# Local attention beside a state-space scan on one core: first tokens loaded in pairs, weight rows loaded twice, 64-row parts paired, one rotation more on VectorE, the last block in halves, and a new order

## The chip, the core and the metric

The kernel runs on one core of a Trainium2 chip. The core has TensorE (PE; its weight loads are listed apart as PEld), VectorE (DVE), ScalarE (ACT), GpSimd (POOL) and SyncE (SP), which here only issues DMAs. The metric is the device time of one execution in microseconds.

## The reference

Two independent parts take their own input of 2048 tokens by 448 features (bf16), and their results stand side by side in the output (2048 x 896).

```python
# A: dilated local attention, 16 heads of 28, window 8, dilation 2
qkv = x @ wqkv                                  # 448 x 1344
logits[s, w] = q[s] . k[s - 2 w] * 28 ** -0.5   # w = 0..7, masked where s - 2 w < 0
o[s] = sum_w softmax(logits[s])[w] * v[s - 2 w]
a = o @ wo
# B: a diagonal complex recurrence (S5)
Lam_bar = exp(dt * Lam);  Bu = x @ (((Lam_bar - 1) / Lam)[:, None] * Bmat).T
h[t] = Lam_bar * h[t - 1] + Bu[t]
b = 2 * real(h @ Cmat.T) + x * Dskip
out = concat(a, b)
```

## The kernel before

**The order.** Every piece of work is a small Python function ("step") with a name and arguments. The string `ORDER` lists all steps by hand, and the loop at the end of the kernel calls them one after the other. A step appends its instructions to the queues of the engines that it uses; within an engine instructions run in that order, and between engines semaphores hold a reader until its input is there and a writer until the old content has been read. `@` and digits give the banks of PSUM (eight, 0 to 7) that a step writes; `.` and `=` at the end say whether a copy out of PSUM (an eviction) runs on ScalarE or VectorE. So `qk010.` is the eviction of step `qk` for u=0, m=1, s=0 on ScalarE. DMAs stand in SP's queue in the same way, ScalarE's three small ones aside; SP stops at a DMA whose input is not ready.

**Part A.** x is brought to `xT` (features on partitions): tokens 0 to 1023 (u=0) by TensorE, `XI` for the first 512 and `XA`, `XH` for the next, with evictions `xi`, `xa`, `xh`; tokens 1024 to 2047 (u=1) by transposing DMAs. 448 features are three chunks of 128 and one of 64. The 64-row chunk of two 512-token halves s=0, 1 lies on partitions 0 to 63 and 64 to 127, so its weights are needed on both: the load brings them to partitions 0 to 63, and POOL copies them to the others and gathers the last heads' columns in `wq6` (lines 213 to 218). `QK(u, m, k)` projects to queries (even m) and keys (odd m) for both halves: k=0 the three full chunks, k=1 the two 64-row parts as a pair on the two halves of the array. `QS(m, s)` does all four chunks of one half, with one 64-row matmul by itself. `qk` and `qh` evict to `qf`, `kf`, `qh_t`, `kh`. `V_`/`v` do the same for the values. `P` forms products of queries and shifted keys on VectorE (24 of `pr<-qf,kf`, 4 of `pr<-qh_t,kh`); `E_` sums them over a head by a matmul with 32 columns of weights; `lt`, `TR`, `tr`, `sma`, `smb`, `smc` are scaling, transpose and softmax; `AL`, `al`, `ad`, `sp` spread the probabilities into a band `PT` through DRAM; `AV`, `av`, `W_`, `w`, `ow` are the weighted sum, the output projection and its store.

**Part B.** Tokens are grouped in fours (T = 4, j = 0..3), states in seven groups g of 64 (real and imaginary part on 128 partitions). `tf`, `ts`, `pa` to `pg`, `rb` compute tables and rotation matrices `R`. `BU` (input projection) and `BR` (adds the step before, rotated) fill PSUM; `z` evicts; `UP`, `sa`, `sb`, `sd`, `DN`, `dn` do the scan over groups of four tokens. Its carry then goes into the tokens j = 0..2 by one of two ways: `H_(j, g)` rotates it on TensorE and `h` adds it on VectorE (12 pairs of j, g), or `sw` copies it across partitions by DMA and `ha`, `hb` (or `ka`, `kb`, the same instructions) rotate and add it on VectorE (9 pairs). `C(j, ct)` multiplies 128 tokens by the output matrix (seven matmuls of 448 columns), `c` adds `x * Dskip`, `oc` stores. The order ends with C01, C02 and the store oc02.

Changes of the array: a weight of 128 rows by 128 columns, of 64 rows, or of 32 columns uses TensorE in different shapes, and the order decides how often the shape changes.

Of the kernel before, what the change touches and what calls it, by code (L numbers as in the profile page):

```python
# [9 lines left out]
BF16 = mybir.dt.bfloat16  # L10
# [5 lines left out]
HALO = 14  # L16
# [21 lines left out]
qh000. qh011. v000= qh101. QK110@70 P010 E_00@4 qh001. E_02 E_04 xt3 ts13 QK111 P031 QK121@31 qh100. QK141@65 qh111.
QK140 hc0 qk111. ts23 qk141. ts25 QK120 qk140. qk120. QK100@05 qk121. P050 qk110. V_410@63 hc1 qh110. QK101 P061 P011
qk100. qk101. V_411 E_01@1 tf2 ts02 P051 LC P030 E_03 tf6 E_05 QK130@72 P060 E_06 QK151@05 v411. v410. QK131 qk130.  # L40
P101 qk131. P111 lt00 P110 QK150 qk151. V_500@36 V_501 qk150. V_511@72 lt01 P131 v501. V_401@45 TR0@0 V_400 ts06 V_510
E_11@1 tr0. P100 v500. v401. v400. v511. v510. P130 E_13 E_10@6 sma0 smb0 P121 P141 BU401@03 OZ P150 BU201@54 BU301@27
# [20 lines left out]
def kernel(  # L63
# [68 lines left out]
    def qk_load(c, n):  # L132
        for a in range(2):
            SP.dma_start(qk_s[:, 0:3, a, c:c + n], qk_d[0:384, a, c:c + n].rearrange("(f p) n -> p f n", p=128))
        SP.dma_start(qk_s[0:64, 3, :, c:c + n], qk_d[384:448, :, c:c + n])
# [784 lines left out]
```

## Time and profile before

| | |
|---|---|
| three runs | 131.55 to 131.69 us, median 131.67 |
| the profiled execution | 131.66 us, of which the span of its instructions 129.9 us |
| busy in the span | PE 123.9 us, DVE 119.0, ACT 90.9, PEld 62.8, POOL 23.0 |
| DMA | 22.91 MB in 44838 packets, 31064 of them under 512 bytes |
| first matmul, end of the last one | 1.06 us, 126.5 us |

Rows of the timeline give start, length, engine, source line, operation, the tile written and read, the shape and the count; in brackets the idle time before and what ended it. Lengths of matmuls overlap, so the cost of one in a dense row is the distance from start to start. Groups give the busy time and the mean length of one in ns. The chain of waits is followed back from the last instruction. SPq is SP's queue with DMA issues.

### The profile page before, as it was taken

How to read it: one execution, taken by the hardware profiler on the slowest of the kernel's cores; microseconds unless marked ns; L12 is line 12 of the kernel's file. 1: busy time of each engine (PE TensorE's matmuls, PEld its weight loads, DVE VectorE, ACT ScalarE, POOL GpSimd, SP SyncE). 2: the span in 40 equal slices, each digit the busy share in tenths (PEclk: the TensorE clock that was granted, in tenths of full speed). 3: DMA queues.
4: the chain of work that ended last, by engine and by line, in shares of the span. 5: the costliest groups of instructions: out<-in, count | busy, mean ns of one | idle time of the engine just before them, and what ended most of it. 6: DMA issues, size and time to landing. Idle time of an engine off the chain costs nothing.

```text
span 129.9 us, 2872 instructions
## 1 busy us (share of the span) xinstructions
PE 123.9 (95%) x1071; PEld 62.8 (48%) x1071; DVE 119.0 (92%) x211; ACT 90.9 (70%) x185; POOL 23.0 (18%) x45
## 2 busy tenths in 40 slices
PE   6899999999989999999999999999999999999990
PEld 6843445343423434435446335945694554555540
DVE  5679999999999999999999999999999999999941
ACT  3459899999974999987999987999889651000000
POOL 6817300000000000003999900000000000000000
PEclk9999999999999999999999999999999999999999
DMA  3899998999999979973577699995512430124463
GB/s 99 196 315 270 308 214 166 229 221 237 167 204 213 226 192 343 240 136 71 203 186 138 273 259 239 209 153 91 184 29 89 110 129 6 34 71 139 144 208 110
DMA packets 44838, 22.91 MB, mean 176 GB/s; under 512 B 31064, under 2 KB 43800, under 8 KB 44824
## 3 DMA queue, kind: packets, MB, share of 16 engines
q1 hardware_dynamic: 44760, 22.72, 74.8%
q8 instruction: 8, 0.13, 0.4%
q14 instruction: 7, 0.05, 0.1%
q10 hardware_dynamic: 63, 0.01, 0.0%
HBM read 11.56 MB, written 6.29 MB: 137 GB/s over the span
## 4 chain that ended last, share of the span: by engine, by line
PE 57%; DVE 28%; ACT 9%; issue 3%; DVEq 0%
PE ps L238 21%; DVE pr L378 13%; PE ps L831 13%; PE ps L524 4%; PE ps L701 4%; PE ps L511 3%; DVE Ak L796 3%; PE ps L256 2%; PE ps L347 2%; DVE Z L800 2%; DVE Z L772 2%; ACT kh L114 2%; ACT qf L114 1%; DVE Cw L667 1%; ACT qh_t L114 1%
## 5 line engine op out<-in xcount | busy, mean ns | idle before, releaser
L378 DVE TENSOR_TENSOR pr<-qf,kf 128x2048 bf16<-128x2048 bf16 x24 | 28.4, 1231 | 0.0
L238 PE MATMUL ps<-xbuf,BT 128*128 128x512 bf16 (+1 forms) x112 | 24.0, 379 | 0.0
L831 PE MATMUL ps<-Cw,Z 128*128 128x448 bf16 x112 | 21.8, 352 | 0.1
L238 PE MATMUL ps<-xT,wq 128*128 128x512 bf16 (+1 forms) x96 | 19.7, 380 | 0.0
L114 ACT CAST Z<-ps 128x512 bf16<-128x512 f32 (+1 forms) x34 | 15.7, 503 | 0.9 <-PE ps L713 0.5
L831 PEld LDWEIGHTS <-Z 128*128 128x128 bf16 x112 | 11.0, 98 | 10.5 <-issue 0.3
L238 PEld LDWEIGHTS <-BT 128*128 128x128 bf16 (+1 forms) x112 | 9.1, 97 | 11.7 <-issue 2.4
L524 PE MATMUL ps<-wo,oT 128*128 128x448 bf16 x64 | 13.6, 353 | 0.0
L238 PEld LDWEIGHTS <-wq 128*128 128x128 bf16 (+1 forms) x96 | 7.5, 97 | 11.5 <-issue 4.0
L238 PE MATMUL ps<-wq,xT 128*128 128x448 bf16 (+1 forms) x64 | 12.0, 353 | 0.0
L877 POOL MEMSET PT<- 128x4320 f32 x3 | 11.0, 3699 | 0.0
L837 DVE TENSOR_TENSOR xbuf<-ps,xnB 128x448 bf16<-128x448 f32 x16 | 9.2, 619 | 2.0 <-PE ps L831 1.7
L114 ACT CAST oT<-ps 128x512 bf16<-128x512 f32 x17 | 9.5, 626 | 1.4 <-PE ps L511 1.4
L114 ACT CAST ya<-ps 128x448 bf16<-128x448 f32 (+1 forms) x17 | 8.4, 557 | 2.8 <-issue 1.6
L663 ACT ACTIVATE ctmp<-Cw,c2t 64x448 f32<-64x448 bf16 x14 | 9.3, 666 | 0.3
L114 ACT CAST kf<-ps 128x512 bf16<-128x512 f32 x12 | 6.8, 596 | 3.5 <-PE ps L238 2.5
L524 PEld LDWEIGHTS <-oT 128*128 128x128 bf16 x64 | 6.1, 98 | 5.7 <-ACT oT L114 0.6
L511 PE MATMUL ps<-PT,v_s 128*32 128x135 bf16 (+1 forms) x256 | 8.4, 299 | 0.0
L238 PEld LDWEIGHTS <-xT 128*128 128x128 bf16 (+1 forms) x64 | 5.3, 97 | 5.5 <-issue 1.1
L772 DVE TENSOR_TENSOR Z<-ps,Z 128x512 bf16<-128x512 f32 x12 | 7.9, 682 | 0.0
L114 ACT CAST v_s<-ps 128x448 bf16<-128x448 f32 x15 | 7.3, 541 | 0.5 <-PE ps L238 0.5
L511 PEld LDWEIGHTS <-v_s 128*32 128x32 bf16 x256 | 7.1, 112 | 0.2 <-issue 0.2
(159 smaller groups left out, 197.0 us busy)
## 6 DMA issues: line engine op xcount, KB each, us to landing
PT<-pd SPq DMA_DIRECT2D x16, 156.0 KB, 4.0
xnB<-in_B_x_dram SPq DMA_DIRECT2D x2, 896.0 KB
out_dram<-ya SPq DMA_DIRECT2D x16, 112.0 KB, 1.7
out_dram<-xbuf SPq DMA_DIRECT2D x16, 112.0 KB, 1.7
pd<-Ak SPq DMA_DIRECT2D x2, 640.0 KB, 3.2
xbuf<-in_A_x_dram SPq DMA_DIRECT2D x2, 448.0 KB
xnB<-in_B_x_dram SPq DMA_DIRECT2D x4, 224.0 KB, 6.0
xnB<-in_B_x_dram SPq DMA_DIRECT2D x4, 192.0 KB, 4.4
```

The lines of the kernel that those rows point to most:

```text
L114: (ACT.copy if e == "A" else V.tensor_copy)(o, i)
L238: PE.matmul(o, l, r, start=(first and i == 0), stop=(not first and i == len(pairs) - 1 and not more[s]))
L378: V.tensor_tensor(t[:], q.unsqueeze(1).to_broadcast((128, 4, 512)), k4, ALU.mult)
L511: PE.matmul(p[32 * hh:32 * hh + 32, 128 * bl:128 * bl + n], v_s[:, t, 4 * hg + hh, :], PT[:, t % NS, (4 * hg + hh) // HS, (4 * hg + hh) % ...
L524: PE.matmul(p[:, 0:D], late["oT"][:, b // 4, hg, par, 128 * (b % 4):128 * (b % 4) + 128], late["wo"][:, hg, :], start=(hg == 0), stop=(hg ...
L663: ACT.activation(t[a:a + 64, 0:D], Cw[b:b + 64, g, :], ACTF.Copy, scale=c2t[a:a + 64, g:g + 1])
L701: PE.matmul(pp["z", g, j][:], rot(g, 0), late["Z"][:, g, j - 1, :], start=False, stop=True)
L772: V.tensor_tensor(zz, pp.pop(("h", j, g))[:], zz, ALU.add)
L796: e.scalar_tensor_tensor(t.rearrange("p (a n) -> p a n", a=2), prev(g), co2[:, 0, j, g:g + 1], late["Z"][:, g, j, :].rearrange("p (a n) -> ...
L831: PE.matmul(p[:, 0:D], z, Cw[:, g, :], start=(g == 0), stop=(g == G - 1))
L837: V.tensor_tensor(yo, pp.pop(("c", j, ct))[:, 0:D], xnB[:, ct, j, :], ALU.add)
L877: POOL.memset(late["PT"][:, 4 * i:4 * i + 4].rearrange("p t g n -> p (t g n)").bitcast(F32), 0.0)
```

## The change

- **Tokens 0 to 1023 of A.** A block of 256 tokens is loaded as 128 partitions of two neighbouring tokens (1792 bytes in one piece) instead of two tiles of 128 tokens. A column n of the i-th transposed half-block is now token 2n + i, so the evictions of queries and keys for u=0 read PSUM in the order (half-block h, n, i) and write tokens in order; the values' weights for u=0 are read in contiguous columns instead of every second.
- **Last 64 weight rows.** `qk_load` brings only the first 384 rows; `half_load` brings the last 64 rows of queries and keys, whole, to partitions 0 to 63 and again to 64 to 127. POOL's four kinds of copies go; step `wc` gathers `wq6` in one copy on ScalarE.
- **64-row parts.** `QA` replaces `QS`: three matmuls, without the 64-row one; `QK(0, m, 1)` finishes m = 0 and 1 as a pair.
- **Rotations.** `ha23`, `hb23` and `sw3` replace `H_23`, `h23`: ten pairs on VectorE, eleven on TensorE.
- **Last block.** C(0, 3) is the last and is done in two halves of 224 columns (`CH`, `ch`, `oh`), columns 224 to 447 first (store issued by SP), columns 0 to 223 last (store issued by ScalarE); `oa` is a store issued by ScalarE (block 0, 0).
- **Order.** `ORDER` is written anew from end to end, with other banks and other engines for some evictions.

```diff
 ORDER = """
-WU@0 XI0@12 xi30. xi00= XI1@3 xi31. xi01= xi20. xi21= PP@4 pcopy pa pb pe pc QS00@5 pd_ QS10@6 qk010. XA10@7 XH1@1
-qk000. xh1. xt1 XA11@0 pf xt2 xa10= xa11= QS11@3 qk011. QK050@24 QK051 tf0 ts00 P000 QK021@65 QK041@70 QK031@13 tf1
+WU@0 XI0@12 PP@3 pcopy xi00. xi20. pa XI1@4 xi01. xi30= pb xi21= QA00@5 BD pc pe XA10@6 pd_ xa10= XH1@7 xt1 XA11@1
+xa11= QA10@3 xi31. QA01@2 xh1. tf5 QA11@0 tf3 QK031@46 QK011 pf pg QK001 QK021@71 wc. qk010. qk011. ts05 QK030 rb1
+QK020 qk000. P000 ts15 P001 V_100@30 ts03 qk001. V_101 qk020. qk021. v100. ts25 QK041@52 V_001@71 rb0 tf0 V_000 qk030.
...
-C22@3 oc21 c23 oc20 kb04 oc23 oc32 ow51 h03 kb06 c33 C11@6 c22 c11 oc11 C00@0 c00 oc00 C03@4 ow61 oc33 c03 oc03 C01@1
-c01 C02@7 oc22 ow40 c02 oc01 oc02
+c22 C23@4 h02 ow61 oc10 c32 ka04 kb05 kb06 kb04 C13@2 c12 c13 oc32 ow40 oc22 c23 C21@0 C00@3 ow51 oc13 c00 oc23 C01@6
+oc12 oa00 c31 oc31 c21 oc21 c01 C02@1 c02 CH1@5 oc01 CH0@2 ch1 oc02 oh1 ch0 oh0
 """
...
+    def half_load(r):
+        SP.dma_start(qk_s[r:r + 64, 3], qk_d[384:448])
...
     def qk_load(c, n):
         for a in range(2):
             SP.dma_start(qk_s[:, 0:3, a, c:c + n], qk_d[0:384, a, c:c + n].rearrange("(f p) n -> p f n", p=128))
-        SP.dma_start(qk_s[0:64, 3, :, c:c + n], qk_d[384:448, :, c:c + n])
-
-    SP.dma_start(xnA[:, 0:2], xA_r[:, 0:2])
-    SP.dma_start(xnA[:, 2:4], xA_r[:, 2:4])
+
+    xb = xbuf.rearrange("p (b n) -> p b n", n=2 * D)
+    xb_r = A_x[0].rearrange("(b p i) d -> p b (i d)", p=128, i=2)
+    SP.dma_start(xb[:, 0], xb_r[:, 0])
+    SP.dma_start(xb[:, 1], xb_r[:, 1])
     qk_load(0, 128)
-    SP.dma_start(xnA[:, 4:8], xA_r[:, 4:8])
+    SP.dma_start(xb[:, 2:4], xb_r[:, 2:4])
     qk_load(128, 320)
+    half_load(0)
+    half_load(64)
...
-    POOL.tensor_copy(qk_s[64:128, 3, :, 0:128], qk_s[0:64, 3, :, 0:128])
-    POOL.tensor_copy(qk_s[64:128, 3, :, 128:384], qk_s[0:64, 3, :, 128:384])
-    POOL.tensor_copy(wq6[:, 0:3], qk_s[:, 0:3, :, 384:D])
-    for s in range(2):
-        POOL.tensor_copy(wq6[64 * s:64 * s + 64, 3], qk_s[0:64, 3, :, 384:D])
...
     def QK(u, m, k):
-        p = two("qk", u, m)
+        p = pp["qk", u, m] if u == 0 and m < 2 else two("qk", u, m)
...
-    def QS(m, s):
+    def QA(m, s):
         p = ps()
         pp.setdefault(("qk", 0, m), {})[s] = p
+        begun.add(("qk", 0, m))
         for kt in range(3):
             PE.matmul(p[:], wqk(m, slice(0, 128), kt), xT[:, 0, 4 * s + kt], start=(kt == 0), stop=False)
-        PE.matmul(p[:], wqk(m, slice(64 * s, 64 * s + 64), 3), xT[64 * s:64 * s + 64, 0, 3], start=False, stop=True)
+
+    @op
+    def wc(e):
+        evict(e, wq6[:], qk_s[:, :, :, 384:D])
+
+    def qk_copy(u, o, i, e):
+        if u == 0:
+            o = o.rearrange("p (h n i) -> p h n i", h=2, i=2)
+            i = i.rearrange("p (h i n) -> p h n i", h=2, i=2)
+        evict(e, o, i)
...
     def V_(b0, par, k):
         p = two("v", b0, par)
         c = 256 * (b0 % 2)
+        c = slice(c + par, c + 256, 2) if b0 >= 4 else slice(c + 128 * par, c + 128 * par + 128)
...
+    @op
+    def oa(j, ct):
+        ACT.dma_start(out_b[j, ct // 2, ct % 2, :, D:2 * D], pp.pop(("yo", j, ct)))
+
+    LAST, CUT = (0, 3), (0, 224, 448)
+
+    @op
+    def CH(i):
+        j, ct = LAST
+        p = pp["ch", i] = ps()
+        n = CUT[i + 1] - CUT[i]
+        for g in range(G):
...
+            PE.matmul(p[:, 0:n], z, Cw[:, g, CUT[i]:CUT[i + 1]], start=(g == 0), stop=(g == G - 1))
+
+    @op
+    def ch(i):
...
+        V.tensor_tensor(yo[:, sl], pp.pop(("ch", i))[:, 0:CUT[i + 1] - CUT[i]], xnB[:, ct, j, sl], ALU.add)
+
+    @op
+    def oh(i):
+        j, ct = LAST
+        (ACT if i == 0 else SP).dma_start(out_b[j, ct // 2, ct % 2, :, D + CUT[i]:D + CUT[i + 1]], pp.pop(("yo", "part", i))[:, CUT[i]:CUT[i + 1]])
```

`qk` and `qh` call `qk_copy` in place of `evict`.

More of the change, by code (lines that the diff above doesn't have):

```diff
@@ L38 @@
[L38 to L42, printed above, removed]
```

60 lines of the change are left out of this document (35 added, 25 removed).

## The prediction, made before the result was known

> **What bounds the kernel now.** I read the page first (busy time, chain), then busy time by stage, then TensorE's instructions in order of time, and last the waits of the first ten microseconds.
>
> ```profile
> span 129.9 us, 2872 instructions
> PE 123.9 (95%) x1071; PEld 62.8 (48%) x1071; DVE 119.0 (92%) x211; ACT 90.9 (70%) x185; POOL 23.0 (18%) x45
> PE 57%; DVE 28%; ACT 9%; issue 3%; DVEq 0%
> ```
>
> The busy time by stage has, after the stage and its length, busy us and count of instructions of PE, its weight loads, DVE, ACT and POOL, then the granted clock, the DMA share and GB/s.
>
> ```profile
> 10.00:40.00 30.00, 29.41 (x198) 11.92 (x197) 29.17 (x52) 26.67 (x59) 3.59 (x8) 1.00 1.14 223
> 93.00:109.00 16.00, 15.97 (x220) 9.56 (x219) 15.81 (x31) 11.65 (x23) 0.00 (x0) 1.00 0.27 81
> 109.00:126.50 17.50, 17.43 (x92) 8.80 (x90) 15.56 (x26) 0.00 (x0) 0.00 (x0) 1.00 0.33 107
> ```
>
> TensorE has 0.6 us free from 10 to 40 and next to nothing after that, at full clock in every row. VectorE is close behind: from 93 to 109 it misses 0.2 us, and it has 1.9 us only in the last stage. So TensorE's own work is the first thing to count, VectorE's the second. ScalarE has 3.3 us free from 10 to 40, which matters for one of the rivals. A "busy" TensorE may still be spaced out, so I take the price of a matmul from the distance between starts.
>
> ```profile
> 61.44 0.38 PE L701 MATMUL ps<-Z,R 128*128 128x512 bf16 x1
> 61.76 0.39 PE L238 MATMUL ps<-xbuf,BT 64*128 64x512 bf16 x2
> 62.08 0.39 PE L701 MATMUL ps<-Z,R 128*128 128x512 bf16 x1
> 62.30 2.75 PE L238 MATMUL ps<-xbuf,BT 128*128 128x512 bf16 x12
> 64.89 0.38 PE L701 MATMUL ps<-Z,R 128*128 128x512 bf16 x1
> ```
>
> Twelve matmuls of 512 columns take 64.89 - 62.30 = 2.59 us, 0.216 each. At 61.76 two matmuls of 64 rows, on the two halves of the array, take 0.32 us together, and the one of 128 rows ahead of them 0.32 too: a pair costs what one does (0.216), and each change between 128 and 64 rows costs 0.10 more.
>
> **The start, where most of the change lies.**
>
> ```profile
> 6.52 0.81 PE L347 MATMUL ps<-xT,wq 128*128 128x512 bf16 x3 [0.42 <-DVE xT L114]
> 7.26 0.39 PE L348 MATMUL ps<-xT,wq 64*128 64x512 bf16 x1
> 7.58 0.82 PE L347 MATMUL ps<-xT,wq 128*128 128x512 bf16 x3
> ...
> 9.11 0.39 PE L320 MATMUL ps<-ident,xbuf 128*128 128x128 bf16 x4
> 9.33 0.39 PE L306 MATMUL ps<-ident,xbuf 128*128 128x128 bf16 x4
> 10.05 0.81 PE L347 MATMUL ps<-xT,wq 128*128 128x512 bf16 x3 [0.33 <-DVE xT L114]
> ```
>
> QS00 (6.52) has four matmuls and takes 1.06 us to the next start, where 4 x 0.216 = 0.864: again 0.10 for each of two changes. Its 64-row matmul is alone and pays like a pair. XA11 starts at 9.33; its four transposes need 0.22 (as the four at 9.11 do), so TensorE could go on at 9.55 and starts QS11 at 10.05: 0.50 us wait for VectorE's copies.
>
> **The change, part by part.**
>
> *64-row parts.* QA leaves the 64-row matmul to QK(0, m, 1), which does it in pairs: four single blocks become two pairs, -2 x 0.216 = -0.43 us of TensorE.
>
> *Fewer changes of array shape.* I walked both instruction orders along TensorE and counted the places where rows x columns of the weights change: 44 before, 37 after (128 to 64 rows or back 26 before, 19 after; the 32-column and tiny ones stay at 18 together). The four pairs QK031, QK011, QK001, QK021 share one change in and out. -7 x 0.10 = -0.70.
>
> *Rotations.* One more rotation (j=2, g=3) goes from TensorE to VectorE: H_ was 12 and is 11, -0.22 on TensorE. VectorE trades one L772 for one L796 and one L800:
>
> ```profile
> L772 DVE TENSOR_TENSOR Z<-ps,Z 128x512 bf16<-128x512 f32 x12 | 7.9, 682 | 0.0
> L800 DVE SCALAR_TENSOR_TENSOR Z<-BT,co,Ak 128x512 bf16<-128x512 bf16 x9 | 6.6, 743 | 0.0
> L796 DVE SCALAR_TENSOR_TENSOR Ak<-Z,co,Z 128x512 f32<-128x512 bf16 x9 | 6.6, 742 | 0.0
> L837 DVE TENSOR_TENSOR xbuf<-ps,xnB 128x448 bf16<-128x448 f32 x16 | 9.2, 619 | 2.0 <-PE ps L831 1.7
> L760 DVE TENSOR_TENSOR Z<-ps,Z 128x256 bf16<-128x256 f32 x7 | 2.8, 419 | 0.3 <-PE ps L754 0.3
> L114 DVE CAST qf<-ps 128x512 bf16<-128x512 f32 x1 | 0.7, 684 | 0.0
> L114 ACT CAST qf<-ps 128x512 bf16<-128x512 f32 x11 | 6.0, 590 | 0.9 <-PE ps L238 0.9
> L114 ACT CAST Z<-ps 128x256 bf16<-128x256 f32 x14 | 4.6, 378 | 0.5 <-PE ps L713 0.5
> ```
>
> That is +0.74 + 0.74 - 0.68 = +0.80. But the new order also moves copies out of PSUM: VectorE had nine and has eight, smaller ones on balance (by the 684 ns row and shorter ones, about -0.95 us in sum), so its total stays within 0.2 us of 119.0, ScalarE's grows by about as much. The two more copies between partitions (sw3) go on SP ahead of later output stores; SP waits for its producers there, so I cost them at nothing; without that cover an issue is 0.6 us.
>
> *Last block halved.* Seven matmuls of 448 columns become fourteen of 224. The last stage has 17.39 us for 91 (chain of waits below), 0.191 each, so 1.34; by columns a half is 0.096, fourteen 1.34. I take 0.00; the 128-column transposes at 9.11 take 0.055 each, a weight load with each, so loads do not hold the halves up. The gain is behind it: the last add is 0.62 us for 448 columns and 0.42 for 256, so about 0.39 for 224.
>
> ```profile
> 109.11 17.39 PE ps L831 x91
> 126.52 0.62 DVE xbuf L837
> out_dram<-xbuf SPq DMA_DIRECT2D x16, 112.0 KB, 1.7
> BT<-Z SPq DMA_DIRECT2D x6, 64.0 KB, 2.4
> ```
>
> -0.23, if the last store lands as before. The half is stored in 448-byte rows and issued by ScalarE; nothing here shows such a store. Its nearest rows are 1.7 us (896-byte rows) and 2.4 (512-byte rows, on chip), so between 0 and +0.7; I take 0, for the destination is that of the 1.7 row. The Trainium skill, "DMA: Bandwidth & Descriptors", Specifications, says that pieces under 512 bytes fall below line rate because they are read, changed and written back. By that page the tail would gain nothing and the sum come out 0.2 us higher; no run here shows a store of that size.
>
> *Loads.* SP's issues at the start, the time to landing of the last, and the first rows of ScalarE and VectorE that follow:
>
> ```profile
> 2.90 0.74 SPq L135 DMA_DIRECT2D wq<-in_A_wqkv_dram  x1
> 3.69 0.58 SPq L140 DMA_DIRECT2D xbuf<-in_A_x_dram  x1
> 5.40 0.62 SPq L135 DMA_DIRECT2D wq<-in_A_wqkv_dram  x1
> wq<-in_A_wqkv_dram SPq DMA_DIRECT2D x1, 80.0 KB, 5.2
> 10.45 1.28 ACT L585 ACT_TABLE_LOAD   x1
> 11.43 1.52 DVE L378 TENSOR_TENSOR pr<-qf,kf 128x2048 bf16<-128x2048 bf16 x1
> ```
>
> The 64-row load ahead of tokens 512 to 1023 is gone, so these are issued 0.79 us earlier (2.90), in half as many packets. XA10 wants them sooner too, near 7.2 us, behind one QA instead of two QS, so this gain is used up. The last weight rows come twice, issued near 4.6 and 5.2 us instead of once at 5.40, and land by the 5.2 us row at 9.8 to 10.4. The first user, QK031, is due at 10.1. ScalarE's copy `wc`, which replaces POOL's four copies, waits for them too and has eight evictions, and thereby VectorE's first products, queued behind it; ScalarE reaches it near 10.5: XH1's copy ends near 8.4, then come the table load of 1.28 us and the sines. Cost 0 to 0.3, I take 0. `tx`, moved behind the last rotations, makes one more such load (1.28) near the end, when only one eviction is left on ScalarE; without that cover it costs its 1.28.
>
> *The wait at 9.55.* After the change QA10 follows XA11 and reads only tokens 0 to 511, so 3 x 0.216 = 0.65 us of TensorE lies beside VectorE's two copies: -0.50. Next is QA01, which needs those copies: QA00 starts as QS00 did (6.5), XA10 ends near 7.65, copies of 0.7 and 0.4 us end near 8.45 and 8.8, QA01 starts near 8.7 with the part that is there. TensorE then reaches QK031 near 10.1.
>
> VectorE must come earlier as well, or TensorE waits at E_. Before its first product it now does the small work (tf5, tf3, pg, rb1) that stood behind; along its order the first product comes 3.2 us of own work later, but at 13.9 us instead of 11.43, so it is about 0.8 us ahead of its old schedule (2.5 us later by the clock, 3.2 by work). So TensorE's 1.35 us can come through.
>
> *Order anew.* The waits inside TensorE's busy time go on: the products' wait is 0.5 us on the page of waits, and a new order may add such. Between 0 and +0.5, I take +0.25, the middle.
>
> ```profile
> PE ps L390 <- DVE pr L378: 0.5, 1, 0.5
> ```
>
> **Sum.** -0.43 - 0.70 - 0.22 = -1.35 of TensorE's work; -0.50 wait; -0.23 tail; +0.25 new waits: -1.83 us. The profiled execution took 131.66 us (span 129.9 and 1.76 around it); the median of the runs shown is 131.67, so no shift: 129.8 us. A measurement of this kernel can tell 0.2% (0.26 us) from no change.
>
> **Rivals.**
>
> *Slower: ScalarE's strided reads.* For the first 1024 tokens the evictions (on ScalarE 11 of 128 rows and 4 of 64, on VectorE one) read PSUM in the order (half, n, i), pairs of columns 128 apart. No row here reads PSUM so. The streaming part of an eviction is (590 - 378)/256 = 0.83 ns a column, 0.42 us of 512; at half rate 15 of them are +6.3 us on ScalarE between 10 and 28 us. From 10 to 40 it has 3.3 us free; the other 3.0 would fall on VectorE's products and so on TensorE: 129.8 + 3.0 = 132.8. It decides from 0.34 us an eviction on ((3.3 + 1.83)/15). For it: ScalarE is the fullest engine just there. Against: the nearest row, its copy of bf16 with blocks swapped (Cn, 896 columns, 943 ns), runs at 1.05 ns a column, and TensorE's writes into PSUM in runs of four below are not slowed. Chance 0.10.
>
> ```profile
> L114 ACT COPY Cn<-Cr 128x896 bf16<-128x896 bf16 x3 | 2.7, 943 | 0.0
> 61.49 0.03 PE ps L458
> ```
>
> The Trainium skill, "Advanced Engine Details and Errata", PSUM Cachelines, speaks for this rival: every two elements in a row should be neighbours for the best throughput. The 64-column writes of 0.03 us keep to that rule, so they do not test it.
>
> *VectorE is the bound.* Its 119.0 us do not shrink; if it starts its products no earlier, TensorE's gain turns into waits for products at E_ and only the tail is left: 131.66 - 0.23 = 131.4. For it: 28% of the chain, 15.81 of 16 us. Against: its 1.9 us idle at the end, and the earlier start. Chance 0.12.
>
> *The last weight rows come late.* Twice 112 KB in 64-row loads; if they land 1 us after 10.4, QK031 and `wc` move and all behind them: 130.8. Chance 0.08.
>
> *The order also closes the old waits* (0.5 at the products, and the 0.25 I added): 129.0. Chance 0.12.
>
> *The forecast*, 129.2 to 130.5: chance 0.58.
>
> Range: leaving about half of the slower rival out and taking the fast one in, 128.8 to 132.2. Faster 0.78 (forecast, late rows, closed waits), same 0.07 (half of VectorE's case), slower 0.15 (strided reads, and the rest of the others).
>
> **What would show it.** Right: L772 x11, TensorE's last matmul ending near 124.9 us (now 109.11 + 17.39 = 126.50), no wait between the transposes and the QA blocks, QK evictions still near 590 ns, the last add near 0.39. Wrong: evictions of kf and qf of 0.8 us or more; a wait of L238 on wq; VectorE's products ending no earlier than now and TensorE waiting at E_; a last store of over 2 us.

## The result, and the profile after

| | before | after |
|---|---|---|
| median of runs on the same chips | 131.61 us (131.09 to 131.87, 12 runs) | 130.75 us (130.16 to 131.60, 12 runs) |
| ratio | | 0.9944, 95% interval 0.9920 to 0.9968 |
| the profiled execution, its span | 131.66, 129.9 us | 130.57, 128.8 us |
| last matmul ends, last add ends | 126.50, 127.14 us | 125.49, 125.90 us |

The change makes the kernel 0.56% faster, 0.74 us by the ratio (0.42 to 1.05). Forecast were 1.83 us. The profiled executions differ by 1.09 us; the readings below account for these 1.09, and no trace shows where the other 0.35 went. The runs after spread over 1.4 us, those before over 0.8.

The page of the kernel after, span, busy time and chain by engine, and then the busy time by stage (columns as in the prediction; the last stage ends with the last matmul):

```profile
span 128.8 us, 2882 instructions
PE 122.0 (95%) x1068; PEld 63.5 (49%) x1077; DVE 119.2 (93%) x212; ACT 94.5 (73%) x188; POOL 19.9 (15%) x40
PE 59%; DVE 19%; ACT 9%; issue 5%; DMA 4%; SPq 1%; DVEq 0%
```

```profile
10.00:40.00 30.00, 29.36 (x199) 12.12 (x201) 28.68 (x49) 28.31 (x64) 0.88 (x4) 1.00 1.12 221
93.00:109.00 16.00, 15.90 (x178) 8.98 (x169) 15.91 (x30) 10.90 (x21) 0.00 (x0) 1.00 0.27 78
109.00:125.50 16.50, 16.48 (x94) 8.97 (x92) 15.96 (x27) 1.66 (x3) 0.00 (x0) 1.00 0.41 132
```

TensorE's busy time fell by 1.9 us, VectorE's did not. A DMA stands in the chain for the first time, with 4%. VectorE, which had 1.9 us free in the last stage, has 0.5 us now.

The start, TensorE's timeline of the kernel after, and from its chain in order of time the piece that stands ahead of it:

```profile
5.54 0.50 PE L289 MATMUL ps<-wz 128*128 128x128 bf16 x6
6.38 0.84 PE L349 MATMUL ps<-xT,wq 128*128 128x512 bf16 x2 [0.34 <-ACT xT L114]
7.63 0.62 PE L307 MATMUL ps<-ident,xbuf 128*128 128x128 bf16 x8 [0.42 <-DMA xbuf<-in_A_x_dram]
8.31 0.39 PE L307 MATMUL ps<-ident,xbuf 128*128 128x128 bf16 x4
8.54 2.10 PE L349 MATMUL ps<-xT,wq 128*128 128x512 bf16 x9
10.57 3.87 PE L239 MATMUL ps<-xT,wq 64*128 64x512 bf16 x20
```

```profile
2.74 4.85 DMA xbuf<-in_A_x_dram
```

QA00 goes at 6.38 (one of its three matmuls is missing from the record) and is done with its 0.65 us at about 7.05. XA10 then waits until 7.63 for the third x load (tokens 512 to 1023), 0.58 us. From XA10 to the first 64-row pair (10.57) there is no gap any more: the wait of 0.50 us between XA11 and QS11 is gone, and a wait of 0.58 us ahead of XA10 has come.

Two more waits are new. TensorE's and VectorE's timelines near 76 us, DN1 and the last scan step that it reads:

```profile
75.77 0.81 PE L239 MATMUL ps<-xbuf,BT 128*128 128x512 bf16 x3
76.79 0.27 PE L767 MATMUL ps<-Z,R 128*128 128x256 bf16 x1 [0.21 <-ACT Z L114]
```

```profile
76.22 0.42 DVE L762 TENSOR_TENSOR Z<-vv,p 128x512 bf16<-128x512 bf16 x1
```

The three matmuls before DN1 take 0.65 us by their 0.216 each, to 76.42; DN1 starts at 76.79, 0.37 us later, behind VectorE's step that ends at 76.64 (and a copy on ScalarE). And near 103.9 us, where the output blocks begin:

```profile
103.49 0.38 PE L780 MATMUL ps<-Z,R 128*128 128x512 bf16 x1
103.89 2.43 PE L844 MATMUL ps<-Cw,Z 128*128 128x448 bf16 x12
```

```profile
103.16 1.88 DVE L785 TENSOR_TENSOR Z<-ps,Z 128x512 bf16<-128x512 f32 x3
```

H_03 takes 0.216, so C31 could go at 103.71 and goes 0.19 later, when h20, the first of the three adds of VectorE, is done and its bank free. From there the sixteen blocks and one H_ follow one another without a gap.

VectorE's first product, which a mark below starts from:

```profile
14.56 2.35 DVE L390 TENSOR_TENSOR pr<-qf,kf 128x2048 bf16<-128x2048 bf16 x2
```

Groups by form, which answer to the terms of the sum:

```profile
L785 DVE TENSOR_TENSOR Z<-ps,Z 128x512 bf16<-128x512 f32 x11 | 7.2, 685 | 0.0
L114 ACT CAST qf<-ps 128x512 bf16<-128x512 f32 x12 | 6.6, 600 | 0.2 <-PE ps L239 0.2
L114 ACT CAST kf<-ps 128x512 bf16<-128x512 f32 x11 | 6.2, 590 | 0.5 <-PE ps L239 0.5
L880 DVE TENSOR_TENSOR xbuf<-ps,xnB 128x224 bf16<-128x224 f32 x2 | 0.8, 391 | 0.3 <-PE ps L872 0.3
```

### The profile page after: what moved, and what is told of

Its sections match the earlier page's. It is cut to its first block, busy times and chain, and to the rows that moved or that the text cites. A ratio compares the mean times of both kernels' runs of the same rounds, so it can differ in the third digit from the quotient of the medians.

```text
span 128.8 us, 2882 instructions
## 1 busy us (share of the span) xinstructions
PE 122.0 (95%) x1068; PEld 63.5 (49%) x1077; DVE 119.2 (93%) x212; ACT 94.5 (73%) x188; POOL 19.9 (15%) x40
## 4 chain that ended last, share of the span: by engine, by line
PE 59%; DVE 19%; ACT 9%; issue 5%; DMA 4%; SPq 1%; DVEq 0%
PE ps L239 19%; DVE pr L390 16%; PE ps L844 16%; PE ps L537 9%; PE ps L524 6%; DMA xbuf<-in_A_x_dram 4%; ACT Z L114 3%; PE ps L714 2%; PE ps L780 2%; PE ps L349 2%; PE ps L872 1%; ACT ctmp L676 1%; ACT L649 1%; ACT ya L114 1%; DVE R L658 1%
## 5 line engine op out<-in xcount | busy, mean ns | idle before, releaser
L239 PE MATMUL ps<-xbuf,BT 128*128 128x512 bf16 (+1 forms) x109 | 23.3, 379 | 0.4 <-issue 0.3
L239 PE MATMUL ps<-xT,wq 128*128 128x512 bf16 (+1 forms) x97 | 20.5, 379 | 0.2
L844 PE MATMUL ps<-Cw,Z 128*128 128x448 bf16 x105 | 20.2, 352 | 0.0
L114 ACT CAST Z<-ps 128x512 bf16<-128x512 f32 (+1 forms) x32 | 14.9, 505 | 2.0 <-PE ps L714 0.9
L844 PEld LDWEIGHTS <-Z 128*128 128x128 bf16 x105 | 10.3, 98 | 9.8 <-issue 0.3
L239 PEld LDWEIGHTS <-wq 128*128 128x128 bf16 (+1 forms) x100 | 8.1, 97 | 10.8 <-issue 2.5
L239 PE MATMUL ps<-wq,xT 128*128 128x448 bf16 (+1 forms) x64 | 12.8, 354 | 0.0
L850 DVE TENSOR_TENSOR xbuf<-ps,xnB 128x448 bf16<-128x448 f32 x15 | 8.6, 627 | 0.2 <-PE ps L844 0.2
L809 DVE SCALAR_TENSOR_TENSOR Ak<-Z,co,Z 128x512 f32<-128x512 bf16 x10 | 7.2, 750 | 0.0
L785 DVE TENSOR_TENSOR Z<-ps,Z 128x512 bf16<-128x512 f32 x11 | 7.2, 685 | 0.0
```

The lines of the kernel that those rows point to most:

```text
L114: (ACT.copy if e == "A" else V.tensor_copy)(o, i)
L239: PE.matmul(o, l, r, start=(first and i == 0), stop=(not first and i == len(pairs) - 1 and not more[s]))
L785: V.tensor_tensor(zz, pp.pop(("h", j, g))[:], zz, ALU.add)
L809: e.scalar_tensor_tensor(t.rearrange("p (a n) -> p a n", a=2), prev(g), co2[:, 0, j, g:g + 1], late["Z"][:, g, j, :].rearrange("p (a n) -> ...
L844: PE.matmul(p[:, 0:D], z, Cw[:, g, :], start=(g == 0), stop=(g == G - 1))
L850: V.tensor_tensor(yo, pp.pop(("c", j, ct))[:, 0:D], xnB[:, ct, j, :], ALU.add)
```

## The experiments

Every kernel below was timed in five rounds against the kernel before. The times stand in one table; the readings come from each kernel's profiled execution.

| kernel | median us (lowest to highest, runs) | ratio to the kernel before, 95% interval |
|---|---|---|
| the change | 130.75 (130.16 to 131.60, 12) | 0.9944 (0.9920 to 0.9968) |
| e1_x_there | 160.74 (160.08 to 162.10, 6) | 1.2221 (1.2178 to 1.2264) |
| e1b_x_there | 130.46 (130.20 to 131.40, 7) | 0.9931 (0.9904 to 0.9957) |
| e2_load_order | 131.00 (130.76 to 131.32, 7) | 0.9952 (0.9935 to 0.9969) |
| e3_rows_once | 131.16 (130.71 to 131.58, 8) | 0.9961 (0.9942 to 0.9981) |
| e4_whole_block | 130.80 (130.58 to 131.42, 6) | 0.9941 (0.9919 to 0.9962) |
| e5_x_first | 130.54 (130.17 to 131.35, 10) | 0.9935 (0.9915 to 0.9956) |
| g1_qa10_first | 130.95 (130.47 to 131.18, 12) | 0.9949 (0.9932 to 0.9966) |
| g4_qa10_xi21 | 130.92 (130.55 to 131.75, 12) | 0.9960 (0.9940 to 0.9981) |
| e6_dn1_later | 131.09 (130.70 to 132.09, 12) | 0.9980 (0.9960 to 1.0001) |
| e7_e06_later | 132.55 (132.23 to 133.46, 6) | 1.0096 (1.0066 to 1.0126) |
| f1_pe_more | 131.45 (130.78 to 132.13, 12) | 0.9989 (0.9967 to 1.0010) |
| f2_dve_more | 130.76 (130.54 to 131.10, 6) | 0.9945 (0.9924 to 0.9966) |
| f3_h23_back | 133.64 (133.18 to 134.22, 5) | 1.0160 (1.0129 to 1.0191) |
| f4_z_on_act | 131.98 (131.36 to 132.36, 12) | 1.0029 (1.0012 to 1.0047) |
| g2_nine_rotations | 130.37 (130.24 to 131.00, 7) | 0.9928 (0.9902 to 0.9954) |
| g3_before_halves | 131.47 (130.97 to 131.95, 12) | 1.0001 (0.9980 to 1.0021) |
| h1_nine_x_first | 130.42 (130.33 to 131.16, 6) | 0.9919 (0.9894 to 0.9944) |

Not all kernels ran on the same chip, and the kernel before had medians from 131.48 to 131.70 beside them; so kernels are compared by their ratios. The intervals are about half a us wide, as wide as most of the differences sought. So the verdicts rest on three marks of each trace: XA10 (the first transpose that needs the third load), TR1 (the transposes `PE L420` near 58 us) and C31 (the first output block, near 104 us). In the kernel after they stand at 7.63, 58.02 and 103.89: 50.39 us from the first to the second, 45.87 from the second to the third.

**The wait at XA10 taken away.** The first kernel read the first tiles for the second 512 tokens:

> Leaves out: the transposes of tokens 512 to 1023 of A read tokens 0 to 511 instead, so XA10 does not wait for the third x load. Everything else is the changed kernel. Theory 1 (the load's landing holds the start, and the start sets the end): the 0.58 us wait at XA10 goes, the first QK block (10.57 us) comes near 10.0 and the time falls by 0.4 to 0.6 us against the changed kernel, to about 130.2. Theory 2 (the twice-loaded 64-row weights are just as late): the first QK block waits for wq instead and still goes at 10.4 to 10.6, time as the changed kernel within 0.15. Theory 3 (the start does not matter, since VectorE's products or later waits set the end): the QK block comes near 10.0, but TensorE waits longer at E_06 (0.68 us now) and the time stays within 0.15.

```diff
-                PE.transpose(..., xnA[:, 4 * b + t, 128 * f:128 * f + 128], ident[:])
+                PE.transpose(..., xnA[:, t, 128 * f:128 * f + 128], ident[:])
```

It took 160.7 us, and tells nothing of the question: `xt1`, which stands between XH1 and XA11 in the order, overwrites these tiles, so XA11 had to wait 28.5 us for part B's transposes. With XA11 ahead of `xt1`:

> Leaves out: the transposes of tokens 512 to 1023 of A read tokens 0 to 511 instead (and XA11 stands before xt1, which overwrites these tiles), so XA10 does not wait for the third x load. Theory 1 (that landing holds the start, and what the start gains reaches the end whole): XA10 goes at about 7.0 instead of 7.63, the first QK block at 10.0 to 10.1 instead of 10.57, the last block and the time 0.4 to 0.6 us earlier, about 130.2. Theory 2 (the 64-row weights are as late): the first QK block still goes at 10.5, waiting for wq; time within 0.15 of the changed kernel. Theory 3 (VectorE or later waits absorb it): first QK block at 10.0, but E_06 waits over 1.0 us instead of 0.68 and the time is within 0.15.

TensorE's timeline of this kernel:

```profile
7.08 0.61 PE L307 MATMUL ps<-ident,xbuf 128*128 128x128 bf16 x8
7.97 2.36 PE L349 MATMUL ps<-xT,wq 128*128 128x512 bf16 x9
57.64 0.61 PE L420 MATMUL ps<-ident,lt 128*128 128x128 bf16 x8
103.52 5.46 PE L844 MATMUL ps<-Cw,Z 128*128 128x448 bf16 x28 [0.22 <-DVE Z L785]
```

XA10 goes 0.55 us earlier. The nine QA matmuls then take 0.26 longer than the 2.10 of the kernel after, since QA01 now waits for VectorE's copies, so 0.31 is left at the first pair. TR1 comes 0.38 and C31 0.37 earlier, and the profiled execution took 130.21 us, 0.36 less. So in the traces theory 1 holds: what the first pair gains reaches the end whole. In time it is not shown: by the ratios it is 0.13% of the kernel before, 0.17 us, within their intervals. This kernel does not wait for the third load, and still its seven runs spread over 1.2 us; so the load's landing is not what spreads the runs, or not alone.

**What the third load waits for.** Three kernels move the loads.

> The two loads of the 64-row weights go ahead of the two loads of the other weight columns (128 to 447). Theory 1 (DMA throughput holds the start: what is issued behind takes bandwidth from what is ahead): tokens 512 to 1023 land 0.2 to 0.5 us earlier than 7.59, the 64-row weights 1 us earlier, the other columns 0.5 us later; the first QK block comes 0.2 to 0.4 earlier unless it now waits for wq, and the time falls by 0 to 0.4. Theory 2 (a load's landing is set by its issue alone): tokens 512 to 1023 land at 7.6 as now, and nothing moves but the order of the weights; time within 0.15.

```diff
-    qk_load(128, 320)
     half_load(0)
     half_load(64)
+    qk_load(128, 320)
```

> The 64-row weights are loaded once, and GpSimd copies them to the other 64 partitions (keys, then queries), as the kernel before did. Theory 1 (the second load's 112 KB cost time in a start that DMA throughput holds): one load fewer ahead of the values' weights, tokens 512 to 1023 land as now or up to 0.2 earlier, and the first QK block goes at 10.3 to 10.6 if GpSimd's copies (about 1.1 us by the 0.39 us for 256 and 0.61 us for 512 columns of the kernel before) end by then; time 0 to -0.3. Theory 2 (loading twice was worth it): the copies end at 10.8 or later, the first QK block waits, and the time rises by 0.2 to 0.5.

```diff
     half_load(0)
-    half_load(64)
+    POOL.tensor_copy(qk_s[64:128, 3, 1], qk_s[0:64, 3, 1])
+    POOL.tensor_copy(qk_s[64:128, 3, 0], qk_s[0:64, 3, 0])
```

> The third x load goes ahead of the first weights (and the 64-row weights ahead of columns 128 to 447), and TensorE does XA10, XH1, XA11 ahead of QA00. Theory 1 (the third load lands late because its packets stand behind 768 weight packets of 256 bytes, which end at 6.0 us): it lands near 5.3 instead of 7.6, XA10 goes at 5.8 to 6.0, QA00 near 6.8, the first QK block near 9.7 to 10.1, and with it the end comes 0.4 to 0.8 us earlier: 130.0 to 130.4. Theory 2 (the sum of all bytes that the first QK block needs sets it, whatever their order): the first QK block waits for wq and goes at 10.4 or later, and the time is within 0.2 of the changed kernel.

```diff
-    qk_load(0, 128)
     SP.dma_start(xb[:, 2:4], xb_r[:, 2:4])
+    qk_load(0, 128)
-    qk_load(128, 320)
     half_load(0)
     half_load(64)
+    qk_load(128, 320)
 ORDER
-QA00@5 BD pc pe XA10@6 pd_ xa10= XH1@7 xt1 XA11@1 xa11= QA10@3
+BD pc pe XA10@6 pd_ xa10= XH1@7 xt1 XA11@1 xa11= QA00@5 QA10@3
```

XA10's row of e2, and of e5:

```profile
7.89 0.62 PE L307 MATMUL ps<-ident,xbuf 128*128 128x128 bf16 x8 [1.06 <-DMA xbuf<-in_A_x_dram]
```

```profile
7.79 0.62 PE L307 MATMUL ps<-ident,xbuf 128*128 128x128 bf16 x8 [1.20 <-DMA xbuf<-in_A_x_dram]
```

In e2 nothing but the two 64-row loads was moved up behind the third x load, in e5 the load itself went a full us earlier, ahead of the weights, and both times it landed near 7.8. The traces also hold the time at which each of the 16 DMA engines reported its share of a load:

| profiled execution of | third load issued | shares reported | XA10 |
|---|---|---|---|
| the kernel after | 2.74 | fourteen from 5.79 to 6.78, then 7.33 and 7.59 | 7.63 |
| e4 (same loads) | 2.72 | sixteen from 6.34 to 7.17 | 7.22 |
| e2 (64-row loads next) | 2.73 | fifteen from 6.49 to 7.56, then 7.85 | 7.89 |
| e5 (ahead of the weights) | 1.72 | eleven from 5.04 to 5.78, four to 6.63, then 7.74 | 7.79 |
| h1 (same loads as e5, below) | 1.72 | sixteen from 5.34 to 6.69 | 6.73 |
| the kernel before | 3.69 | sixteen from 6.90 to 8.22 | 8.65, no wait |

TensorE waits for the slowest of sixteen. Thirteen profiled executions have the loads of the kernel after, and their last share came at 7.15 to 8.10. e2's, at 7.85, is one among these: one execution shows no gain from its order. e5 is not so simple. Issued a us earlier, fifteen of its shares were there by 6.63, where the thirteen take until 7.04 to 7.84; only the last was late. In h1, with the same loads, all were there by 6.69, earlier than in any of the thirteen, though not near the 5.3 of theory 1. So the place ahead of the weights does bring the load earlier, by up to a us, and one late share can undo it; how often, two executions cannot say. (e5's profiled execution, 131.11 us, is also among the slowest of its ten runs, 130.17 to 131.35.)

Single packets are of the size to account for a late share: a 256-byte packet of the weights takes 0.02 us and a 1792-byte packet of x 0.09 us in the mean, but in each of these executions nine to some twenty packets between 3.4 and 6.6 us took 0.2 to 0.9 us (in the kernel after 0.80 at 4.25, 0.85 at 4.88). That an engine which meets one or two of them is the late one is argued, not shown, for the packets do not carry their engine, and h1 has as many of them as e5; what holds such a packet no trace here shows. In the kernel before the same load could land as late as 8.65 without cost.

In e3 GpSimd's copies came too late, as its theory 2 had it: they start when the single load has landed and end at 11.72. Its rows on GpSimd:

```profile
10.42 0.60 POOL L219 COPY wq<-wq 64x448 bf16<-64x448 bf16 x1 [4.01 <-DMA wq<-in_A_wqkv_dram]
10.97 0.75 POOL L220 COPY wq<-wq 64x448 bf16<-64x448 bf16 x1
```

The pairs behind the first one started 0.3 to 0.6 later than in the kernel after, and C31 at 104.39, 0.50 later. XA10 was 0.12 later to begin with, so loading the rows twice is worth some 0.4 us here.

**QA10 ahead of XA10**, so that TensorE has work while the load lands:

> QA10 goes ahead of XA10, as QS10 stood in the kernel before, so that TensorE has 0.65 us of work while the third x load lands. Theory 1 (the start is held by the slowest DMA engine's share of that load, 7.2 to 8.0 us in the runs so far): XA10 goes at 7.7 to 8.0 with no or little wait for the load, QA01 then waits up to 0.5 us for VectorE's copies, the first QK block comes at 10.3 to 10.6, the time is within 0.2 of the changed kernel, and the runs spread less. Theory 2 (the prediction: the copies' wait was worth 0.5 us and its place decides): the first QK block comes 0.5 later, at 11.0, and the time rises by 0.4 to 0.5 us.

```diff
-QA00@5 BD pc pe XA10@6 ... xa11= QA10@3 xi31.
+QA00@5 QA10@3 BD pc pe XA10@6 ... xa11= xi31.
```

> As the kernel with QA10 ahead of XA10, and VectorE's copy xi21 ahead of the three small steps of pb, so that QA00's third matmul does not wait 0.25 us for it. Theory 1 (the third load and the copies behind it hold the start): XA10 goes when the load is there, within 0.2 us of the kernel with QA10 first. Theory 2 (TensorE's own work holds it): the first QK block comes 0.2 earlier than in that kernel, and the time falls by 0.2.

```diff
-xi30= pb xi21=
+xi30= xi21= pb
```

TensorE's timeline of g1:

```profile
5.99 1.52 PE L349 MATMUL ps<-xT,wq 128*128 128x512 bf16 x6 [0.38 <-ACT xT L114]
7.54 0.62 PE L307 MATMUL ps<-ident,xbuf 128*128 128x128 bf16 x8
8.94 1.45 PE L349 MATMUL ps<-xT,wq 128*128 128x512 bf16 x6 [0.34 <-DVE xT L114]
```

The load is there when TensorE comes, and the wait is back in front of VectorE's copies: the transposes end at 8.44 and QA01 starts at 8.94, 0.50 us, the very wait that the change removed. Its time is that of the change (0.9949 against 0.9944). Its runs spread over 0.7 us instead of 1.4, but those of g4, with the same edit and one more, over 1.2, so a narrower spread is not shown. g4 did no better (XA10 at 7.86, first pair at 10.64). So the place of this wait was never worth 0.5 us: the load and the chain of copies behind it end near the same time, whichever of them TensorE stands at.

**Does TensorE's or VectorE's time set the end?** Four kernels put work on one engine or take it off.

> Four more matmuls of 512 columns (0.86 us of TensorE by 0.216 each) ahead of BU210, near 58 us; their result is overwritten. Theory 1 (TensorE is the bound from there, as the prediction's sum takes it): +0.86 us on the last block and the time. Theory 2 (VectorE is the bound from its first product to h20, and TensorE only from C31 on): TensorE's waits of 0.37 us at DN1 and 0.19 at C31 take up part, so +0.3 to +0.5 us.

```diff
     def BU(g, jp, k):
         p = two("bu", g, jp)
+        if (g, jp, k) == (2, 1, 0):
+            for _ in range(4):
+                PE.matmul(p[0][:], BT[:, g, 0, :], xTB[:, jp, 0, :], start=True, stop=True)
```

TensorE's timeline of f1 has the load late (XA10 at 8.03), and TR1 as much:

```profile
58.43 0.61 PE L420 MATMUL ps<-ident,lt 128*128 128x128 bf16 x8
104.77 5.46 PE L847 MATMUL ps<-Cw,Z 128*128 128x448 bf16 x28
```

From TR1 to C31 it takes 46.34 us instead of 45.87: of 0.86 us put in, 0.47 come out, as theory 2 said. The rest is taken up by the waits at DN1 and C31, which are gone in f1. So of TensorE's work added here about half counts.

> VectorE does the copy z02 twice (0.60 us more near 69 us). Theory 1 (TensorE is the bound, VectorE has slack): under +0.2 us. Theory 2 (VectorE is the bound from its first product to h20): C31 waits 0.6 us longer, +0.6 us on the last block and the time.

```diff
         if j < T - 1:
+            if (g, j) == (0, 2):
+                evict(e, late["Z"][:, g, j, :], pp["z", g, j][:])
             evict(e, late["Z"][:, g, j, :], pp.pop(("z", g, j))[:])
```

From TR1 to C31 46.04 us, 0.17 more for the 0.60 put in. But this says nothing of VectorE's slack, because an operation beside it became shorter. VectorE's first step of tf6, in the kernel after and in f2:

```profile
69.69 1.15 DVE L633 TENSOR_SCALAR kM<-iot,fT 128x256 int32<-128x256 f32 x1
```

```profile
70.66 0.45 DVE L633 TENSOR_SCALAR kM<-iot,fT 128x256 int32<-128x256 f32 x1
```

It ends shortly after GpSimd's last zeroing of `PT` (63.35 to 70.69 in the kernel after) in both, so the added copy seems only to have filled time that this step would have stood. f2 is inconclusive.

> The copies z22 and z02 go from VectorE to ScalarE: VectorE -1.2 us between 60 and 69 us, ScalarE +1.0. Theory 1 (TensorE is the bound): within 0.15 us, or slower if ScalarE's copies now hold TensorE. Theory 2 (VectorE is the bound from its first product to h20): VectorE reaches the scan 0.4 to 1.2 earlier, the waits at DN1 and C31 go, and the time falls by 0.3 to 0.6 us.

```diff
-z33. z22= ... z02= al1.
+z33. z22. ... z02. al1.
```

Theory 2 gave the wrong sign: 132.0 us. On ScalarE the copies came later, VectorE stood 1.75 us waiting for ScalarE's `ctmp`, which is queued behind them, and TR1 to C31 took 1.1 us more. ScalarE had no room there, so the question stayed open. It was settled by taking away a rotation:

> The tenth rotation undone: H_23 and h23 in place of sw3, ha23 and hb23. TensorE +0.22 us, VectorE -0.80. Theory 1 (TensorE is the bound, the prediction's term): +0.22 us. Theory 2 (VectorE is the bound up to h20): h20 comes about 0.0 to 0.1 earlier only, since h23 (0.60) stands where ha23 (0.66) stood, but TensorE has no longer the 0.19 us wait at C31 to give; 0 to +0.2 us. If both are equal bounds the tenth rotation was worth nothing: within 0.1.

```diff
-dn3 sw3 ... h22 ha23 AV101@0 ha14 cs4 H_12@5 H_11@3 ha25 ... av101. h11 sw5 ... ow50 hb23 C33@4
+dn3 ... h22 AV101@0 ha14 cs4 H_12@5 H_11@3 H_23@1 ha25 ... av101. h11 h23 sw5 ... ow50 C33@4
```

> The tenth rotation undone again, with H_23 on bank 5 behind C30 and h23 behind hb24, so that DN6 does not wait for it. TensorE +0.22 us, VectorE -0.80. Theory 1 (the prediction's term): +0.22 us. Theory 2 (C31 waits 0.19 us for h20 on VectorE, which now comes 0.66 earlier): C31 goes 0.19 earlier and H_23 costs 0.22 behind it, so within 0.1 us: the tenth rotation was worth nothing.

```diff
-dn3 sw3 ... h22 ha23 AV101@0 ... ow50 hb23 C33@4 hb14 hb26 hb24
+dn3 ... h22 AV101@0 ... ow50 H_23@5 C33@4 hb14 hb26 hb24 h23
```

f3, with H_23 on bank 1 and h23 behind h11, made DN6 wait 2.65 us for that bank and took 133.6 us: a new wait of its own, no reading of the rotation. g2 has no such wait. TensorE's timeline of g2:

```profile
58.33 0.61 PE L420 MATMUL ps<-ident,lt 128*128 128x128 bf16 x8
103.84 2.81 PE L844 MATMUL ps<-Cw,Z 128*128 128x448 bf16 x14
106.49 0.38 PE L780 MATMUL ps<-Z,R 128*128 128x512 bf16 x1
```

From TR1 to C31 it takes 45.51 us, 0.36 less than the kernel after, with no wait at C31; then H_23 (the row at 106.49) takes 0.22 of it back. So with 0.22 us more of TensorE's work and 0.80 less of VectorE's the blocks end 0.14 us earlier. In the middle of the kernel VectorE's work up to h20 sets when the output blocks begin. The stretch before TR1 says the same. From VectorE's first product (14.56 in the kernel after) to TR1 it takes 43.45 to 43.52 us in eleven of the sixteen kernels with the new order (e1 aside), and among them are e4, e6 and f4, in which TensorE stood 0.2 to 0.5 us near 23 us: TensorE's wait there did not move TR1. g2's time is 0.9928 of the kernel before, not separable from the 0.9944 of the change.

**The waits in the middle.**

> DN1 goes behind BU610 in TensorE's order, so that TensorE does not stand at it (0.37 us at 76.2, for the scan's last step on VectorE at 76.64 and the copy z42 on ScalarE). Theory 1 (TensorE's waits go to the end whole): the wait goes, the time falls by 0.3 to 0.4 us against the changed kernel. Theory 2 (VectorE is the bound from there on): TensorE's next waits grow by as much, time within 0.15.

```diff
-BU600 DN1@2 z52. ... DN0@5 BU610 ca1
+BU600 z52. ... DN0@5 BU610 DN1@2 ca1
```

VectorE's and TensorE's rows of e6:

```profile
78.86 0.76 DVE L773 TENSOR_TENSOR Z<-ps,Z 128x256 bf16<-128x256 f32 x2 [0.36 <-PE ps L767]
```

```profile
104.36 0.35 PE L844 MATMUL ps<-Cw,Z 128*128 128x448 bf16 x1 [0.26 <-DVE Z L785]
```

TensorE no longer stands at DN1, but the add that needs DN1 does, 0.36 us on VectorE, everything on VectorE behind it is 0.45 later, and C31 goes 0.47 later with the same start. So it is theory 2's bound, VectorE, though not its time (within 0.15): moving DN1 did not give TensorE's wait back, and 0.4 us more on VectorE cost all of it, 0.36% by the ratios.

> E_06, which waits 0.68 us for VectorE's product, goes behind V_500 and QK150, and TR0 behind V_410 and V_411. Theory 1 (TensorE's waits go to the end whole): the wait goes, and the time falls by 0.5 to 0.7 us. Theory 2 (VectorE's products are the bound there, or ScalarE's copies now come later): the wait turns up again at a later E_ step (E_11 or E_16) or at V_410, and the time is within 0.2 of the changed kernel.

```diff
-qk111. P110 E_06 lt01 qh110. lt00 V_500@76 QK150 XR TR0@4 qk150. P101 qk151. tr0. ts12 V_410@21 V_411 V_501
+qk111. P110 qh110. V_500@76 QK150 E_06 lt01 lt00 XR qk150. P101 qk151. ts12 V_410@21 V_411 TR0@4 tr0. V_501
```

1.8 us slower than the change, which neither theory had: V_500 then waits for its banks (0.55 us, behind ScalarE's copies), V_410 for ScalarE's scaling of the sums (0.72), and VectorE idles 1.7 us between 40 and 60 us instead of 0.5, waiting for TensorE's and ScalarE's steps. The old wait of 0.68 us at E_06 is not free time that an order gives back that simply.

**The tail.**

> The last block (0, 3) is done whole: one C, one add of 448 columns, one store by SyncE. Theory 1 (the prediction's sum): the last add is 0.62 instead of 0.39 us, the store ends as soon after it as now, so +0.23 us. Theory 2 (the store of half rows gives part of it back): from the end of the last add to the end of the span 2.76 us as in the kernel before instead of 2.9, so +0.1.

```diff
-C02@1 c02 CH1@5 oc01 CH0@2 ch1 oc02 oh1 ch0 oh0
+C02@1 c02 C03@5 oc01 c03 oc02 oc03
```

> The kernel before, with its last block (0, 2) alone done in two halves as in the changed kernel. Theory 1 (the prediction: the last add is 0.39 instead of 0.62 us, the store lands as soon): from the start of the last block to the end 0.23 to 0.30 us less, time -0.2 to -0.3 us against the kernel before. Theory 2 (448-byte rows or ScalarE's issue make the store slower): the store lands 0.2 to 0.7 us later after the last add, time 0 to +0.4 us.

```diff
-C01@1 c01 C02@7 oc22 ow40 c02 oc01 oc02
+C01@1 c01 CH1@7 oc22 ow40 CH0@0 ch1 oc01 oh1 ch0 oh0
```

g3 is the kernel before with nothing but the halves, so its diff is against that kernel; `CH`, `ch` and `oh` are those of the change. From the first matmul of the last block to the last share of the last store it takes 3.58 us with halves in the kernel after (123.97 to 127.55) and 3.85 with the whole block in e4 (123.64 to 127.49): the halves give 0.27. e4's runs do not show it (0.9941 against 0.9944); in its profiled execution the load landed early, and XA10 at 7.22 makes up for it. In the kernel before the same halves give nothing, in time (1.0001) as in the trace: 3.86 us from the last block to the landing in both. VectorE's last row of g3 and its SP queue:

```profile
125.86 0.39 DVE L862 TENSOR_TENSOR xbuf<-ps,xnB 128x224 bf16<-128x224 f32 x1 [0.28 <-PE ps L854]
```

```profile
125.24 0.43 SPq L534 DMA_DIRECT2D out_dram<-ya  x1
125.78 0.39 SPq L841 DMA_DIRECT2D out_dram<-xbuf  x1
126.27 0.40 SPq L867 DMA_DIRECT2D out_dram<-xbuf  x1
```

The last add ends 0.22 earlier against the block's start, but the last landing comes 0.21 later against the add (1.92 us instead of 1.71). What lands last, at 128.17, is the store of the first half: its add ended at 125.58, but SP, which has the stores of other blocks ahead of it, issues it only at 126.27. The second half's store, issued by ScalarE, landed 0.19 earlier. In the kernel after SP issues the first half's store at 125.26, right behind its add, and the second half's lands last, 1.65 us after its add. So the halves pay only where SP's queue is free by then.

**Both edits together.**

> Both edits that the runs point to: the third x load ahead of the weights with XA10, XH1, XA11 ahead of QA00, and nine rotations on VectorE. If the effects add (the first kernel measured 0.9935 of the kernel before, the second 0.9928, the changed kernel 0.9944): 0.991 to 0.993, some 130.3 to 130.5 us, 0.2 to 0.4 below the changed kernel. If the start's gain is only run-to-run spread of the load's landing: as the nine rotations alone.

The edits are those of e5 and g2.

0.9919 of the kernel before, the lowest ratio here, 0.25% under the change, with overlapping intervals; I do not claim that it is faster. TensorE's rows of h1:

```profile
6.73 0.62 PE L307 MATMUL ps<-ident,xbuf 128*128 128x128 bf16 x8 [0.72 <-DMA xbuf<-in_A_x_dram]
24.39 1.99 PE L239 MATMUL ps<-xT,wq 128*128 128x512 bf16 x10 [1.25 <-DMA xT<-xbuf]
```

XA10 goes 0.90 earlier than in the kernel after, but the first pair is only 0.10 earlier (all twelve QA matmuls now stand behind the transposes). At 24.39 us TensorE has stood 1.25 us for the transposing DMAs of tokens 1024 to 2047, which SP issued from 16.85 on instead of 15.12, and TR1 comes 0.5 later than in the kernel after. This execution (131.16 us) is the slowest of the six, four of which took 130.33 to 130.46; whether those had this wait no trace shows.

## Why the prediction was right or wrong, point by point

- **The sign and the range**: 130.75 us lies within 128.8 to 132.2, and faster was the likeliest. The size is wrong: 0.74 us of 1.83.
- **TensorE's work, -1.35**: held, as far as a subtraction shows it. The last matmul ends 1.01 us earlier (125.49 against 126.50) with 0.50 us of wait removed and 1.14 of waits added (0.58, 0.37 and 0.19, below), so the rest fell by about 1.65; 0.14 of that is QA00's earlier start (6.38 against 6.52), which leaves 1.5 for work and small waits. The records have seven changes of shape fewer, as counted (35 instead of 42 from 6 us on), the 64-row pairs of 0.216 us stand in the first rows behind 10.57, and H_ is eleven times there.
- **The failed step is the pair "wait at 9.55, -0.50" and "new waits, +0.25".** I wrote of the third load that XA10 "wants them sooner too, near 7.2 us, behind one QA instead of two QS, so this gain is used up", and so took the load as just in time without a row that shows its landing. It lands at 7.6 in this execution and at 7.2 to 8.1 in others with the same loads, 4.4 to 5.4 us after its issue where the kernel before took 4.5: 0.58 us of wait ahead of XA10, more than the 0.50 taken away. The first pair, which I had near 10.1, goes at 10.57, and at 10.26 in e1b, which does not wait for the load. With the two waits for VectorE (0.37 at DN1, 0.19 at C31) the new waits come to 1.14 instead of 0.25. These 0.9 us, less the 0.3 of the point above, and some 0.1 more from the last add to the end of the span are the 0.7 by which the profiled executions (1.09) fall short of the 1.83. That the runs fall short by another 0.35 stays open.
- **That the start's gain reaches the end**: right in the traces, but by way of VectorE. XA10 to TR1 takes 50.4 us in the kernel after, in e2, e4 and f1 alike, and C31 moves by as much; where it takes longer (e1b and g2 50.6, e3 and e5 50.8) copies, weights or the QA blocks came late, and in e1b and e3 the time from VectorE's first product to TR1 is still the same 43.5. So the landing of one load is in the time of the execution, where the kernel before had 0.4 us of room in its profiled one. Whether it also widens the spread of the runs is open (e1b and g4 above).
- **VectorE must come earlier, "0.8 us ahead of its old schedule"**: wrong in size. The first product started at 14.56 instead of 13.9, so VectorE is 0.1 us ahead by the same count. **VectorE as the bound**, given 0.12, is largely what happened between the first product and h20: g2 and e6 show it. I priced this rival at 131.4 because I let all of TensorE's gain turn into waits at E_; in fact VectorE also had 1.9 us idle in its last stage to give, and gave 1.4 of them. Ahead of its first product it gave nothing: from 4 us on it idles 2.0 there in both kernels.
- **The tenth rotation, -0.22**: nothing. It lowers TensorE's work by that, but adds 0.80 to the engine that sets C31; undone, the blocks end 0.14 earlier against TR1 (g2), too little to show in the times.
- **The tail, -0.23**: mechanism and size right in place (0.27 by the trace, e4 against the change), though in the kernel before it would have given 0 (g3). By the Trainium skill, "DMA: Bandwidth & Descriptors", Specifications, stores under 512 bytes a piece should lose it again through read, change and write back. The trace shows only a small part of that: a 448-byte piece takes 0.025 us and an 896-byte one 0.043 in the mean, a seventh more by the byte, and the half store lands 1.65 us after its add, a whole one 1.70 (e4).
- **Strided reads of PSUM, the rival of 132.8**: did not come about. The copies of `kf` and `qf` on ScalarE take 590 and 600 ns in the mean, as before; single ones take 0.57 to 0.63 us for tokens 0 to 1023 (strided) and 0.57 to 0.64 for the others. By the Trainium skill, "Advanced Engine Details and Errata", PSUM Cachelines, reads that leave pairs apart lose throughput; here they do not, with 0.59 us for 512 columns either way.
- **Late 64-row weights**: no wait in the kernel after, but close: the second copy of them lands at 10.67 and the first pair goes at 10.57 on the first. In g2's execution TensorE waited 0.19 us for them.

## What to carry to other kernels

When the start is full of loads, a load is as late as the last of its shares: look up when that one was there, in more than one execution, and leave the consumer room for the spread, or the time carries it. Where two engines are over 90% busy, take from the one whose work the next stage waits for: work moved from TensorE to VectorE was worth nothing that the times show here, although TensorE was the fuller by share of the span. A wait is not a gain to be had; it is worth only the distance to what stands next behind it, and undoing the change's wait with QA10 showed the same time with the wait in another place.

## What the runs showed of the hardware

- One load's 16 shares land up to 2.7 us apart (5.04 to 7.74 us in e5), and among the packets of that time single ones take 0.2 to 0.9 us instead of 0.02 to 0.09. With the same loads the last share came at 7.74 in one execution and at 6.69 in another (e5, h1).
- A VectorE step of 256 columns (`tensor_scalar`, f32 to int32) that takes 0.35 us at 17.84 took 1.15 us while GpSimd zeroed 128 x 4320 f32 beside it, and ended 0.15 us after that; the bf16 steps around it kept their length (0.68 us for `L680`).
- A matmul of 224 columns starts every 0.096 us, half of the 0.189 us of 448 columns with the same weight load ahead of it: halving this block costs TensorE nothing.
